# A new order of instructions for an adaptive-layer-norm block: the conditioning chain ahead of x1's statistics

## The chip, the cores and the metric

The kernel runs on one core of one Trainium2 chip. A core has five engines with a queue of instructions each: TensorE (PE in the profile; its weight loads are PEld), VectorE (DVE), ScalarE (ACT), GpSimd (POOL) and SyncE (SP), which here only issues DMA transfers. An engine works through its queue in order and waits at semaphores. The metric is the time of one execution on the device in microseconds (us).

## The reference

One transformer block with adaptive layer norm, on x of 2048 rows by 640, all in bf16:

```python
mod = (silu(c) @ w_mod).reshape(1, 6, 1, -1)          # c 1x640, w_mod 640x3840
sa, ca, ga, sb, cb, gb = (mod[:, i] for i in range(6))
h = layernorm(x) * (1 + ca) + sa
x = x + ga * attention(h)      # 32 heads of 20, causal, window 256, then @ wo
h = layernorm(x) * (1 + cb) + sb
x = x + gb * (sigmoid(h @ w_gate) * (h @ w_up)) @ w_down     # inner width 1536
```

Nothing of x can be modulated before c, the six products with w_mod and their way into per-partition or broadcast form are done: this is the conditioning chain.

## The kernel before, in words

x is worked on in eight chunks `a` of 256 rows, each of two blocks of 128 rows. For each chunk: load x; statistics and normalization (`ln_stats`, on VectorE, with the power on POOL; the normalization is L796); turning to hT, by TensorE for chunks 0 and 1 and by transposing DMAs (`transp_dma`, L803) afterwards; modulation of hT (`modulate`, L812, L813, L820, L821); projections to q, k and v (all plain matmuls are issued at L679, those with a tile position at L680); evacuation of q and k into a staging tile `stg` (four buffers; L895, L896) and transposing DMAs from there into QT and KT; scores, exp on ScalarE (L1016 for an edge set, L1042 for a main set), masks on POOL (L1051), the PV matmuls; normalization of the result through two stream transposes on VectorE (L1136, L1145), a trip through DRAM (`doc`) into oT; output projection, residual, second layer norm, transposing DMAs into h2T, its modulation, MLP and second residual. The gates ga and gb are multiplied into `wo` (L1316) and `wd`, the down weights (L1253, twelve slices, VectorE or POOL), once they have come back as a broadcast tile `gbc` through DRAM: gout writes the row, gin reads it back into all partitions. `gbc` holds first ga, then gb.

In the head, TensorE first runs warm-up matmuls on a zeroed tile (`warm`, L660). c arrives as a row, is turned by a matmul (ctr), halved (c_col, L646), put through tanh on ScalarE (cth, L647), becomes siluc on VectorE (L648) and silubc, repeated over columns (L651). `modA` then multiplies silubc with five slices of w_mod (wm0, held in the buffer of `wd`) in ten 64-column matmuls each; VectorE copies the result to mA (L759), and modulation of hT can begin. Between those products stand a few `fill` matmuls (L671).

**What sets the order.** Every operation is an `Op` with a list of allowed engines, a duration, dependences and, for a DMA, a size and a latency. The order is not computed at build time: the list `PLAN` holds one code for each operation, five times the operation's number plus the number of the engine (pe, act, dve, pool, sp). `schedule` walks it, puts each operation at the end of its engine's queue and keeps a model of time as it goes; the model decides which buffer of a pool a tile gets. `emit` then writes each engine's queue in that order, with a semaphore wait where a dependence crosses engines. So durations, latencies and the constants `DSAFE`, `MIXED` and `FETCH` reach the chip only through PLAN and through the choice of buffers. `DSAFE` is added, in the model, to the time from a DMA's landing to its use. A DMA on SP waits for its inputs at the head of SP's queue, and what stands behind it waits too.

Of the kernel before, what the change touches and what calls it, by code (L numbers as in the profile page):

```python
# [348 lines left out]
def c_pe(n):  # L349
# [4 lines left out]
    28, 222, 225, 81, 43, 33, 3, 258, 230, 8, 195, 13, 260, 89, 347, 352, 235, 240, 245, 250, 202, 357, 378, 91, 362,  # L354
    367, 372, 206, 212, 383, 388, 217, 397, 415, 104, 405, 411, 99, 109, 265, 114, 119, 275, 280, 129, 62, 393, 270,
    402, 430, 436, 68, 440, 447, 285, 426, 295, 305, 312, 461, 476, 452, 144, 124, 134, 149, 491, 290, 139, 457, 467,
    300, 420, 154, 472, 487, 482, 515, 23, 58, 520, 496, 615, 620, 526, 540, 546, 767, 600, 627, 500, 505, 511, 762,
    772, 777, 782, 787, 605, 611, 550, 555, 561, 530, 536, 73, 630, 637, 650, 565, 570, 576, 580, 655, 793, 798, 807,
    590, 802, 586, 640, 18, 1625, 850, 596, 662, 680, 665, 670, 1631, 1229, 174, 647, 159, 857, 840, 53, 687, 677,
    846, 700, 705, 712, 810, 48, 1640, 1646, 830, 1234, 179, 715, 730, 735, 78, 817, 837, 1242, 1237, 1257, 820, 1252,  # L360
    745, 826, 750, 756, 1247, 1638, 720, 1655, 1661, 169, 1262, 742, 727, 860, 865, 872, 925, 690, 696, 1653, 164,
    1120, 1529, 1268, 1534, 1273, 1287, 1537, 1725, 890, 1278, 1731, 930, 936, 1127, 1542, 1142, 875, 880, 897, 1552,
    1668, 910, 915, 887, 1557, 1740, 1746, 922, 1547, 1562, 1670, 1682, 1677, 960, 950, 965, 971, 957, 940, 1687,
    1755, 975, 1283, 946, 990, 1146, 1738, 997, 1568, 1010, 1015, 980, 1025, 319, 1761, 1060, 339, 1573, 1578, 1022,
    1040, 1753, 1046, 1587, 1134, 1154, 1299, 1692, 1030, 1036, 1294, 1322, 1065, 1071, 2805, 2811, 987, 1000, 1006,
    344, 194, 1105, 1110, 1583, 189, 1050, 1697, 1117, 1768, 1057, 1075, 1080, 2815, 1087, 1090, 2821, 900, 907, 1316,
    1311, 1308, 2838, 1303, 1770, 1782, 1777, 1139, 184, 1714, 1704, 1095, 2843, 1325, 1102, 1787, 2845, 2851, 1195,
    1202, 1217, 1395, 1400, 1340, 2833, 1406, 1345, 1719, 1709, 2709, 1351, 2868, 2873, 1172, 1495, 1792, 2875, 1375,
    1500, 1360, 2881, 1177, 1506, 1365, 1797, 1380, 1330, 2905, 2911, 1159, 1465, 1594, 1599, 2704, 1724, 1804, 1814,
    2903, 1387, 1337, 2732, 2727, 2898, 1470, 2863, 1510, 1430, 1435, 1515, 1522, 1476, 2888, 2933, 1441, 2928, 2935,  # L370
    1410, 1445, 1450, 1480, 2893, 2858, 2918, 2923, 2828, 2717, 1372, 1809, 1485, 2941, 1616, 1491, 1601, 2712, 1457,
    2722, 2737, 1415, 2945, 1182, 1187, 1192, 2743, 2748, 1819, 329, 1209, 1824, 1825, 1421, 1855, 2977, 1606, 1860,
    1867, 1621, 1830, 1837, 1974, 1359, 1870, 1875, 2951, 1840, 1845, 1611, 2982, 2987, 1464, 3025, 3031, 2500, 2505,
    1882, 1902, 1394, 2515, 2520, 2526, 2535, 1852, 2763, 2768, 38, 2753, 1429, 2779, 1989, 2550, 2540, 2758, 1221,
    3048, 2968, 1907, 1887, 2973, 1892, 1897, 2555, 2562, 1912, 2585, 2590, 2511, 3043, 2546, 2685, 2655, 2597, 2570,
    2958, 2690, 2696, 3055, 2963, 2575, 2992, 2582, 3078, 2620, 2625, 2632, 1918, 2774, 1923, 1927, 1932, 2605, 3061,
    2610, 2670, 2782, 2534, 2787, 2640, 2645, 3085, 3083, 3113, 2652, 2569, 2616, 2675, 2660, 2791, 2801, 3073, 3108,
    3220, 3053, 2796, 2682, 3235, 3225, 2604, 3091, 2639, 1214, 3038, 3103, 3098, 3068, 2667, 1944, 1939, 3240, 324,
    3246, 3231, 3130, 3135, 2997, 3009, 3115, 3120, 3127, 3420, 3150, 3165, 3155, 3162, 2037, 1992, 3141, 3426, 3170,
    3176, 3200, 3205, 1997, 1947, 3430, 3211, 3467, 1951, 1961, 1958, 1967, 3185, 3285, 3290, 2042, 3297, 3458, 3453,  # L380
    3462, 2047, 2002, 2075, 2080, 2085, 2090, 2095, 2050, 2055, 2060, 2065, 2070, 3436, 3448, 2110, 2115, 2120, 3472,
    3477, 1979, 2007, 2125, 2101, 2130, 4105, 4133, 3004, 4128, 2161, 2135, 2140, 2145, 3014, 1164, 1169, 3019, 2150,
    4111, 3255, 2155, 3319, 334, 3324, 1984, 4584, 3190, 3260, 3266, 2107, 2167, 2012, 4135, 4158, 4141, 3482, 3494,
    4163, 4579, 2170, 2195, 2175, 2200, 2205, 3504, 2210, 2180, 4123, 2185, 2190, 2215, 3489, 2221, 3197, 4165, 3327,
    2227, 3347, 3342, 3352, 3332, 3337, 2255, 2260, 3300, 2265, 4607, 4171, 4602, 3270, 3275, 3281, 4153, 4188, 4193,
    4148, 3443, 3305, 3311, 4178, 3499, 3358, 4183, 4118, 3363, 3368, 4195, 2230, 2235, 2240, 2270, 2245, 3378, 2275,
    2250, 2290, 4201, 2281, 2295, 2300, 2305, 2310, 2341, 4205, 4211, 4592, 2315, 2320, 2287, 3373, 2325, 3383, 2330,
# [983 lines left out]
```

## Time and profile before

| | us |
|---|---|
| three timed runs | 326.62, 326.90, 328.47 |
| median | 326.9 |
| profiled execution | 330.35 |
| its span, first to last instruction | 328.6 |
| PE / DVE / ACT / POOL busy in it | 320.4 / 204.5 / 212.8 / 187.6 |
| mean granted TensorE clock | 0.995 |

Where the profile is a page of sums, a row of a group gives line, engine, operation, destination and sources, count, busy time, mean duration and the idle time ahead of it with what ended it. A row of the timeline gives the start from the beginning of the span, the length, and the same names; in brackets stand the idle time before it and who ended that. SPq and ACTq are DMA issues. A busy TensorE is not TensorE at its peak: ends of matmuls are modelled, and warm-up and fill matmuls count as busy.

### The profile page before, as it was taken

The numbers are of one execution on the slowest core, as the hardware profiler recorded it, in microseconds if no ns is written. First come the engines' busy times: TensorE is split into PE (matmuls) and PEld (weight loads), VectorE is DVE, ScalarE is ACT, GpSimd is POOL, SyncE is SP. The second block draws the span as 40 slices with busy tenths as digits, with TensorE's granted clock in tenths as the row PEclk, the third lists the DMA queues.
The fourth block names the chain that finished last, engine by engine and source line by source line (L and its number), as shares of the span: only waits on it lengthen the run. The fifth ranks groups of instructions, "written<-read, shape, count | busy, mean of one in ns | idle before, by whom it ended". The sixth has DMA issues, their size and how long they took to land.

```text
span 328.6 us, 11961 instructions
## 1 busy us (share of the span) xinstructions
PE 320.4 (97%) x5045; PEld 239.7 (73%) x5045; DVE 204.5 (62%) x421; ACT 212.8 (65%) x229; POOL 187.6 (57%) x325
## 2 busy tenths in 40 slices
PE   5999999989999999999999999999999999999996
PEld 2666766666777777776777778777888777887885
DVE  4589878549776666874476637463846366745422
ACT  1589999586977667877586767585686667220220
POOL 3148777564967767867675665748572859201000
PEclk9899999999999999999999999999999999999999
DMA  7996989999763562424553211374030213122201
GB/s 246 372 323 167 308 167 218 161 150 349 207 92 70 115 142 67 94 63 108 128 77 60 56 25 28 61 119 119 16 90 19 65 42 77 28 60 41 82 0 42
DMA packets 73007, 38.20 MB, mean 116 GB/s; under 512 B 46586, under 2 KB 71674, under 8 KB 72954
## 3 DMA queue, kind: packets, MB, share of 16 engines
q1 hardware_dynamic: 71936, 36.29, 46.7%
q10 hardware_dynamic: 1018, 1.15, 1.1%
q8 instruction: 40, 0.66, 0.8%
q14 instruction: 13, 0.11, 0.1%
HBM read 21.30 MB, written 5.25 MB: 81 GB/s over the span
## 4 chain that ended last, share of the span: by engine, by line
PE 89%; DMA 7%; DVE 2%; issue 1%; ACT 1%; SPq 0%; ACTq 0%; DVEq 0%
PE M L679 73%; PE S L680 8%; PE M L680 6%; DMA QT<-stg 2%; DMA hT<-x 2%; DMA gbc<-gate 2%; DMA x<-in_A_x_dram 1%; PE S L679 1%; ACT E L1016 1%; PE S L671 1%; SPq L803 0%; DVE V L896 0%; DVE wd L1253 0%; DVE st L774 0%; DVE T L1136 0%
## 5 line engine op out<-in xcount | busy, mean ns | idle before, releaser
L1051 POOL TENSOR_SCALAR_AFFINE_SELECT E<-E 128x512 bf16<-128x512 bf16 x224 | 141.8, 664 | 63.7 <-PE S L680 23.5
L1042 ACT ACTIVATE E<-S 128x2048 bf16<-128x2048 f32 x56 | 105.0, 1875 | 35.4 <-PE S L680 34.2
L679 PE MATMUL M<-h2T,wu 128*128 128x256 bf16 x480 | 70.5, 273 | 0.5 <-DVE T L1136 0.5
L679 PE MATMUL M<-h2T,wg 128*128 128x256 bf16 x480 | 65.6, 273 | 0.0
L679 PE MATMUL M<-wd,hh 128*128 128x320 bf16 (+2 forms) x396 | 56.9, 295 | 0.0
L679 PEld LDWEIGHTS M<-h2T,wu 128*128 128x128 bf16 x480 | 44.8, 98 | 9.1 <-DVE T L1136 0.8
L679 PEld LDWEIGHTS M<-h2T,wg 128*128 128x128 bf16 x480 | 46.0, 98 | 6.7
L1270 ACT ACTIVATE sig<-M 128x512 f32<-128x512 f32 x48 | 28.2, 596 | 32.1 <-PE M L679 31.0
L1272 DVE SCALAR_TENSOR_TENSOR hh<-sig,M 128x512 bf16<-128x512 f32 x48 | 32.2, 678 | 26.6 <-ACT sig L1270 17.4
L679 PEld LDWEIGHTS M<-wd,hh 128*128 128x128 bf16 x396 | 37.3, 98 | 14.0
L1291 DVE TENSOR_TENSOR x<-M,x 128x320 bf16<-128x320 f32 (+2 forms) x33 | 15.5, 480 | 35.4 <-PE M L679 35.1
L680 PE MATMUL S<-QT,KT 20*64 20x64 bf16 (+4 forms) x1856 | 34.9, 211 | 0.1
L680 PEld LDWEIGHTS S<-QT,KT 20*128 20x128 bf16 (+1 forms) x1856 | 22.1, 98 | 17.6 <-issue 9.2
L1016 ACT ACTIVATE E<-S 128x2048 bf16<-128x2048 f32 x14 | 26.3, 1877 | 10.2 <-PE S L680 10.2
L774 DVE BATCH_NORM_STATS2 st<-x 128x6 f32<-128x320 bf16 x64 | 28.6, 478 | 3.5 <-DMA x<-in_A_x_dram 3.2
L1136 DVE STREAM_TRANSPOSE T<-M 128x512 f32<-128x512 f32 x32 | 21.6, 700 | 14.5 <-PE S L680 13.5
L679 PE MATMUL M<-wk,hT 128*128 128x320 bf16 x160 | 26.6, 299 | 1.1 <-DVE V L896 1.1
L679 PE MATMUL M<-wq,hT 128*128 128x320 bf16 x160 | 26.9, 299 | 0.6 <-DMA QT<-stg 0.5
L679 PE MATMUL M<-wv,hT 128*128 128x320 bf16 x160 | 27.2, 300 | 0.0
L679 PE MATMUL M<-wo,oT 128*128 128x320 bf16 x160 | 25.4, 299 | 0.0
L680 PE MATMUL M<-E,V 128*32 128x256 bf16 (+1 forms) x960 | 23.0, 246 | 0.1
L680 PEld LDWEIGHTS M<-E,V 128*32 128x32 bf16 x960 | 19.1, 97 | 4.3 <-issue 2.7
(82 smaller groups left out, 321.5 us busy)
## 6 DMA issues: line engine op xcount, KB each, us to landing
x<-in_A_x_dram SPq DMA_DIRECT2D x23, 160.0 KB, 3.7
doc<-On SPq DMA_DIRECT2D x64, 40.0 KB
wd<-in_w_mod_dram SPq DMA_DIRECT2D x6, 320.0 KB
wd<-in_B_w_down_dram SPq DMA_DIRECT2D x4, 480.0 KB
out_dram<-x SPq DMA_DIRECT2D x11, 160.0 KB, 2.1
wu<-in_w_mod_dram SPq DMA_DIRECT2D x5, 320.0 KB, 6.7
oT<-doc SPq DMA_DIRECT2D x8, 192.0 KB, 2.7
wg<-in_B_w_gate_dram SPq DMA_DIRECT2D x2, 576.0 KB
```

Source lines behind the costliest of these rows:

```text
L671: ins = e.matmul(p_S.aps[0][:, 3, :], Eall[:, 0:128], Eall[:, 128:640], start=True, stop=True)
L679: return e.matmul(o, l, r, start=st, stop=sp, skip_group_check=True)
L680: return e.matmul(o, l, r, start=st, stop=sp, tile_position=tp, skip_group_check=True)
L774: A("dve", lambda e, g, bi=bi, j=j: e.bn_stats(v(bi * 12 + j * 6, 6), src[bi].ap[:, j * 320:(j + 1) * 320]), 0.48, reads=[src[bi].r()], wr ...
L1016: A("act", lambda e, eng: e.activation(G.ap[:], Sp.ap[:], ACT.Exp, scale=SM_SCALE), 1.876, reads=[Sp.r()], writes=[G.r()], prio=3, tag=f"e ...
L1042: A("act", lambda e, eng: e.activation(wide()[:, :, 64:320], Sp.ap[:].rearrange("p j (t c) -> p (j t) c", c=256), ACT.Exp, scale=SM_SCALE) ...
L1051: A("pool", lambda e, eng, ap=ap, inp=inp, pat=pat, base=base, cm=cm: e.affine_select(ap(), inp(), pattern=pat, compare_op=ALU.is_ge, fill ...
L1136: A("dve", lambda e, g, h=h: e.transpose(T1.ap[:, 512 * h:512 * h + 512], X[h].ap), 0.694, reads=[X[h].r()], writes=[T1.r(h)], prio=3.5, t ...
L1270: A("act", lambda e, g, pg=pg, sg=sg: e.activation(sg.ap[:], pg.ap[:], ACT.Tanh, scale=0.5), c_act(512), reads=[pg.r()], writes=[sg.r()], ...
L1272: A("dve", lambda e, g, pu=pu, sg=sg, f0=f0: e.scalar_tensor_tensor(out=hh.ap[:, f0:f0 + 2, :], in0=sg.ap[:].rearrange("p (a b) -> p a b", ...
L1291: A("dve", lambda e, g, ps=ps, bi=bi, c0=c0, n=n: e.tensor_tensor(x1[bi].ap[:, c0:c0 + n], ps.ap[:, 0:n], x1[bi].ap[:, c0:c0 + n], op=ALU. ...
```

## The change

All 2134 operations stay as they are; three warm-up operations are added (nine instead of six, seventeen matmuls of 512 columns instead of eleven), so the numbers of later operations move by three. The model's figures are altered, and PLAN is replaced by another list for them:

```diff
 PLAN = [
-    28, 222, 225, 81, 43, 33, 3, 258, 230, 8, 195, 13, 260, 89, 347, 352, 235, ...
+    13, 222, 225, 81, 3, 8, 273, 275, 89, 362, 104, 195, 367, 202, 372, 393, ...
...
-DSAFE = 0.2
+DSAFE = 1.0
...
 FETCH = [
-    4.30, 15.19, 23.69, 31.86, ...
+    -5, 15.19, 23.69, 31.86, ...
...
-            dlat=2.95 if pool is p_x1 and b < 4 else 2.24)
+            dlat=(2.95, 4.6, 2.95, 2.95)[b] if pool is p_x1 and b < 4 else 2.24)
...
-                    (2.2 if hi - lo == 640 else 1.12), writes=..., prio=prio, tag=k)
+                    (2.2 if hi - lo == 640 else 1.12), writes=..., prio=prio, tag=k,
+                tmin=2.4)
...
-    load_bulk(wm_ap[0], wm_src[:, :, 0:1280], Rm[0], 0.88, 0.2, "wm0", dlat=2.89)
+    load_bulk(wm_ap[0], wm_src[:, :, 0:1280], Rm[0], 0.88, 0.2, "wm0", dlat=4.0)
...
-    for i in range(6):
-        o = A("pe", warm if i < 5 else lambda e, g: warm(e, g, 1), 1.03 if i < 5 else 0.52, ...)
+    for i in range(9):
+        o = A("pe", warm if i < 8 else lambda e, g: warm(e, g, 1), 1.03 if i < 3 else 0.6 if i < 8 else 0.3, ...)
...
-        last["s"] = [with_pv(f"edge{a}", sc, 0.36, rd, [G, Sp], before, 3)]
+        last["s"] = [with_pv(f"edge{a}", sc, 0.54, rd, [G, Sp], before, 3)]
```

The codes of PLAN, turned back into names, give the queues. Those that the text below speaks of (number behind a name: chunk; x0, x1: blocks of chunk 0; qkt: a transpose from stg into QT or KT; atr, btr: transposes into hT and h2T; amodu, bmodu: their modulations; wds: one scaling of wd):

```
VectorE, head
  before: stats x0, c_col, aggr x0, stats x1, aggr x1, siluc, silubc, norm x0, memset, norm x1, hT evac, mA, modulations
  after:  stats x0, c_col, aggr x0, memset, siluc, silubc, norm x0, stats x1, aggr x1, memset, hT evac, norm x1, mA, modulations
TensorE, head
  before: warm x2, ctr, ident product, warm x4, turn x0, modA 0 1, fills, turn x1, modA 2 3 4, fills, projections
  after:  warm, ident product, ctr, warm x5, turn x0, warm, modA 0 1, warm x2, modA 2, fill, turn x1 (part), fill, modA 3 4, fill, turn x1 (rest), fills, projections
POOL, modulations of chunk 0:  before none;  after two of the ten
SP, ahead of the first gate row
  before: x6, x7, wg0 first part, wm3 first part, gout 0, wu0 first part, atr2, atr2, wm3 second part, wm2, wm2, gin 0
  after:  x6, x7, wm3, wm3, wg1 first part, gout 0, wu0 first part, atr2, atr2, wm2, wm2, gin 0
SP, from oT of chunk 0 on
  before: oT0, wd0, qkt2 x4, atr4, wd3, atr4, qkt3 x4, gin 1, btr0, btr0, wg0 rest
  after:  oT0, qkt2 x2, wd0, qkt2 x2, atr4, atr4, gin 1, qkt3, wd3, qkt3 x3, btr0, btr0, wg0 rest
ACT, modulations of chunk 4:  before three of five (DVE two);  after all five
x10, x11, x13 loads:  before issued by SP;  after by ACT
wds:  before all twelve on DVE;  after nine on DVE, three on POOL (2 and 3 among chunk 2's first masks, 7 later)
```

Instructions listed for ScalarE go from 236 to 230, for VectorE from 421 to 429, for POOL from 313 to 310, for SP from 205 to 206.

More of the change, by code (lines that the diff above doesn't have):

```diff
@@ L628, in load_w3 @@
             dma(lambda lo=lo, hi=hi: W3[k][:, :, lo:hi], lambda lo=lo, hi=hi: wqkv_src[:, :, i * D + lo:i * D + hi],
-                    (2.2 if hi - lo == 640 else 1.12), writes=[R_w3[k][lo // 320]] if halves else R_w3[k], prio=prio, tag=k)
+                    (2.2 if hi - lo == 640 else 1.12), writes=[R_w3[k][lo // 320]] if halves else R_w3[k], prio=prio, tag=k,
+                tmin=2.4)
     x0 = {}
@@ L662, in build @@
     wprev = []
-    for i in range(6):
-        o = A("pe", warm if i < 5 else lambda e, g: warm(e, g, 1), 1.03 if i < 5 else 0.52, prio=90, reads=[R_z], extra=wprev, tag="warm", writes=[R("w")])
+    for i in range(9):
+        o = A("pe", warm if i < 8 else lambda e, g: warm(e, g, 1), 1.03 if i < 3 else 0.6 if i < 8 else 0.3, prio=90, reads=[R_z], extra=wprev, tag="warm", writes=[R("w")])
         wprev = [o]
```

227 rows, old and new, of tables (FETCH, PLAN) are left out of this document.

## The prediction

> **What bounds the kernel now.** I read the page first, then the list of waits by engine, then sums over stretches, then the chain of waits and the timeline where those pointed.
>
> ```profile
> span 328.6 us, 11961 instructions
> ...
> PE 320.4 (97%) x5045; PEld 239.7 (73%) x5045; DVE 204.5 (62%) x421; ACT 212.8 (65%) x229; POOL 187.6 (57%) x325
> ...
> PEclk9899999999999999999999999999999999999999
> DMA  7996989999763562424553211374030213122201
> ```
>
> TensorE carries the time: 320.4 of 328.6 us, and the only digit of its clock row below 9 is the second, 8.2 to 16.4 us. DMA is busy at 0.6 to 0.9 for the first ten slices (82 us) and slack afterwards. Where TensorE is idle at all, the sums over stretches tell (stretch, its length, busy time of PE, PEld, DVE, ACT, POOL with counts, granted clock, DMA share, GB/s), and the waits name who ended it:
>
> ```profile
> 4.30:5.50 1.20, 1.20 (x6) 0.39 (x4) 0.04 (x1) 0.11 (x1) 0.82 (x2) 1.00 0.94 361
> 5.50:7.70 2.20, 0.09 (x2) 0.04 (x2) 2.06 (x7) 0.00 (x0) 0.23 (x1) 1.00 1.01 361
> 7.70:11.00 3.30, 3.30 (x39) 2.75 (x40) 0.69 (x3) 0.84 (x2) 1.00 (x2) 0.50 1.09 355
> 49.00:77.00 28.00, 25.80 (x427) 17.44 (x415) 19.03 (x45) 21.02 (x30) 16.98 (x31) 1.00 1.06 192
> 77.00:326.00 249.00, 249.00 (x3916) 192.18 (x3914) 148.18 (x287) 155.35 (x152) 142.44 (x234) 1.00 0.35 79
> ```
> ```profile
> PE M L679 <- DVE x L796: 2.1, 1, 2.1
> PE S L660 <- DVE E L655: 1.3, 1, 1.3
> PE M L679 <- DVE V L896: 1.1, 1, 1.1
> PE M L679 <- DMA QT<-stg: 0.5, 1, 0.5
> PE M L679 <- DVE T L1136: 0.5, 1, 0.5
> ```
>
> So there are two places to win. In the head TensorE idles 2.1 us for the normalized x0, and then runs 3.30 us at half clock. Between 49 and 77 us it idles 2.2 us in three waits. After 77 us it is busy in 249.00 of 249.00 us: there only the amount of matmul work counts, and a new plan can only lose.
>
> **The change part by part.** The constants (margin after a landing, edge cost, landing times, prefetch table) act only through the order of instructions that PLAN lists; the sole new instructions are six 512-column warm-up matmuls. Every cost is a matter of order.
>
> *Head.* The rows of before:
>
> ```profile
> 1.24 2.31 SPq L574 DMA_DIRECT2D wd<-in_w_mod_dram  x5
> ...
> 1.38 0.37 ACTq L574 DMA_DIRECT2D x<-in_A_x_dram  x1
> ...
> 3.21 0.89 DVE L774 BATCH_NORM_STATS2 st<-x 128x6 f32<-128x320 bf16 x2 [1.97 <-DMA x<-in_A_x_dram]
> ...
> 4.20 0.21 ACT L647 ACTIVATE cth<-c_col 128x5 f32<-128x5 bf16 x1 [1.14 <-DVE c_col L646]
> ...
> 4.75 0.58 POOL L783 TENSOR_TENSOR st<-st,mhalf 128x1 f32<-128x1 f32 x1
> ...
> 5.57 0.89 DVE L774 BATCH_NORM_STATS2 st<-x 128x6 f32<-128x320 bf16 x2 [1.22 <-DMA x<-in_A_x_dram]
> ...
> 6.62 0.11 DVE L648 SCALAR_TENSOR_TENSOR siluc<-cth,c_col 128x5 bf16<-128x5 f32 x1
> 6.76 0.49 DVE L651 COPY silubc<-siluc 128x320 bf16<-128x320 bf16 x1
> ...
> 7.17 0.44 DVE L796 TENSOR_SCALAR x<-x,st 128x640 bf16<-128x640 bf16 x1
> ...
> 7.66 0.71 PE L679 MATMUL M<-ident,x 128*128 128x128 bf16 x5 [2.11 <-DVE x L796]
> ...
> 8.17 1.27 PE L679 MATMUL S<-silubc,wd 128*128 128x64 bf16 x20
> ...
> 11.92 0.17 DVE L759 COPY mA<-S 128x10 f32<-128x10 f32 x1 [0.63 <-PE S L679]
> ...
> 12.76 1.47 PE L679 MATMUL M<-wq,hT 128*128 128x320 bf16 x8
> ```
>
> VectorE waits until 5.57 for x1, with siluc, silubc and the normalization of x0 queued behind x1's statistics, though their inputs (cth at 4.41, x0's power at 5.33) are there. In the new order they come first: siluc 4.5, silubc done 5.1, x0 5.4 to 5.85, and x0's transposes at 5.9 instead of 7.66. The six added warm-up matmuls (1.2 us, as the six of the row 4.30:5.50) stand behind x0's transposes and the first two slices of the modulation product, where TensorE would wait for x1 anyway. x1's statistics slip from 5.57 to 5.85 and end at 7.0; two small steps on POOL and its normalization follow by 8.5, ahead of the last slices: no loss.
>
> What ends last then is w_mod's fifth slice. x0, x1 and five slices are 1.97 MB; at the 361 GB/s of these rows, with the first bytes about 2.3 us in, they have moved at 7.8, and a landing is seen some 1.5 us later (estimate 9.4, from x0: 160 KB issued at 0.79, seen at 3.21). The last two slices' twenty matmuls take half of that 1.27 at full clock, so mA is copied near 10.2, and by the 0.84 us from mA to the first projection, that one comes at 11.2 (range 11.0 to 11.6, as one modulation moves to POOL behind another): 1.5 us earlier than 12.76.
>
> But that price holds for an execution that lost its clock. A before without the half-clock stretch finds the same last slice and gains about 0.1. The three times, 326.62, 326.90 and 328.47, lie 1.6 to 1.8 us apart, about half of the 3.30 us; I therefore take the median run as one that mostly kept its clock. Ends 0.1 and 1.5; I take **-0.4**, nearer the low end by two times of three.
>
> The rule beside this row: the Trainium skill, "TensorE: Matmul & The Clock Gate", section "What's actually happening", drops the clock after at least one idle window of about 3.4 us. The trace disagrees: here 2.2 us with 0.09 busy, after 1.20 fully busy, were enough. By the rule the clock would not have dropped, the head would gain 0.1, and the sum would be 324.8.
>
> *Middle, 49 to 77 us.* The chain of waits (start, length, what), and the timeline of SP, VectorE, ScalarE and TensorE there:
>
> ```profile
> 49.33 7.33 DMA QT<-stg
> ...
> 59.64 6.33 DMA hT<-x
> ...
> 69.10 5.02 DMA gbc<-gate
> ```
> ```profile
> 59.01 0.59 SPq L574 DMA_DIRECT2D wd<-in_B_w_down_dram  x1
> 59.64 3.41 SPq L803 DMA_TRANSPOSE hT<-x  x1
> 63.59 1.24 SPq L803 DMA_TRANSPOSE QT<-stg  x1
> ```
> ```profile
> 65.99 1.58 ACT L820 ACTIVATE hT<-hT,mA 128x256 bf16<-128x256 bf16 x3 [1.74 <-DMA hT<-x]
> ...
> 67.09 1.52 PE L679 MATMUL M<-wk,hT 128*128 128x320 bf16 x10 [1.11 <-DVE V L896]
> ...
> 74.21 1.42 DVE L1253 TENSOR_TENSOR wd<-wd,gbc 128x640 bf16<-128x640 bf16 x3 [1.96 <-DMA gbc<-gate]
> ```
>
> First wait (0.5, at 56.79): chunk 3's projection wants a staging buffer back from chunk 2's transpose, which was issued behind a 480 KB slice of w_down and took 7.33 us. The new order issues two of the four transposes ahead of that slice. Second (1.1, at 67.09): hT of chunk 4 has one transpose ahead of the next w_down slice and one behind; the latter takes 6.33 us and ends just before the modulation at 65.99. The new order has both ahead. Third (0.5, at 76.57): VectorE stands for gbc with the scaling of w_down at the head of its queue, h2T's modulation behind. The new order issues that gate row before chunk 3's transposes, some 6 us earlier against TensorE's work, so the stand disappears. All three gone: **-2.2**, by the stretch row.
>
> *What comes back.* (a) The w_down slice now lies between the first and second transposes of chunk 3, so chunk 4's second projection wants a buffer that lands behind it. Issue to landing behind such a slice is 6 to 7 us in the rows above; with the slice issued near 57 the buffer comes at 64.5 to 65.2, and TensorE asks at 65.0 in the same frame: 0 to 1.0. (b) All five modulations of chunk 4 are now on ScalarE (three, in 1.58, before), 2.6 us in series. Counting the matmuls that stand ahead of it in the new order, TensorE comes to chunk 4's first projection near 63.2 in this execution's frame (67.09 less 1.5 of the head, less the waits before it, and some matmuls now behind it); the modulations are covered while hT lands by 60.5, and with both transposes ahead of the slice I expect 58 to 59. (c) Three of the twelve scalings of w_down go to POOL, two of them among the masks of chunk 2. No row has that form there:
>
> ```profile
> L1253 DVE TENSOR_TENSOR wd<-wd,gbc x12: 426/485/934, 74.2 to 96.5; 128x640 bf16<-128x640 bf16 x12
> ```
> ```profile
> L793 POOL TENSOR_SCALAR x<-x,st 128x640 bf16<-128x640 bf16 x6 | 5.2, 873 | 2.2 <-PE M L679 1.9 <-POOL st L788 0.3
> ```
>
> At least 0.87, at most about four of VectorE's 0.485; I take 1.4, nearer the low row as both read bf16. With it two scalings, 2.8 us, fit among the masks with about 0.7 to spare before chunk 2's first PV matmuls: 0 to 0.8 lost. The Trainium skill ("GPSIMD Engine Reference", section "4.1 Engine selection") puts an elementwise operation of two inputs at about twice VectorE's time: 1.0 here as an estimate, nothing of (c) comes back then, and the sum would be 324.3; no row shows it. Of (a) to (c), 0 to 3, I take **+0.2**.
>
> Three DMA issues for later x blocks move from SP to ScalarE near 60 to 66 us, at the 0.37 of x1's issue each; ScalarE waits 1.74 for hT there, which covers them, else 1.2 is lost. SP's gate row near 25 us gets one more transfer ahead of it: its wait there is for a VectorE result, DMA drains less meanwhile, and no wait of TensorE in the list hangs on the transposes of chunk 2 behind it: 0. Everything after 77 us shifts as a whole: 0, with a loss of up to 0.3 where the last chunk's way from output projection to MLP has about 0.9 us less of TensorE's work in between.
>
> **Sum.** The profiled execution took 330.35, 1.75 outside its span and 3.45 above the median of the runs; the same differences are set against the median: 326.9 - 0.4 - 2.2 + 0.2 = **324.5**.
>
> **The rivals.** *The waits move, they do not go.* The queue of transfers, at share 1.06 from 49 to 77 us, sets these landings, not the order; TensorE then waits its 2.2 elsewhere: 326.5. For it: the share. Against: each wait hangs on one transfer behind one slice. *Slower, by (b).* If hT of chunk 4 lands later than 60.5 in the new run, each us is a us of TensorE, since five modulations in series follow; from a landing at 62.9 the whole gain of 2.4 is spent, and at 65.7, about where it lands now, the time is 324.5 + 5.2 = 329.7. For it: 6.33 us for that one transpose. Against: both are now ahead of the slice. *The head pays in full.* If the median run did lose its clock: 326.9 - 1.5 - 2.2 + 0.2 = 323.4.
>
> **How the numbers follow.** Forecast 0.53, head in full 0.15, waits move 0.20, slower 0.12. A measurement here tells 0.5% (1.6 us) from no change. Faster by more (under 325.3): 0.53 and 0.15, 0.68. Within: 0.20. Slower (over 328.5): 0.12. The range of 8 in 10 runs from 322.4 (head in full, nothing comes back, the last slice 0.8 sooner than estimated) to 327.0 (waits moved, with 0.5 for (c)). The forecast's own range is 323.2 to 325.3.
>
> **What would show it.** Right: siluc before x1's statistics, x0's transposes near 5.9, no half clock from 7.7 to 11, first projection near 11.2; between 49 and 72 us TensorE idle under 1 us, no stand for gbc, first matmul of chunk 0's MLP 3 to 4.5 us earlier than 76.57. Wrong: half clock again in the head (a stretch too idle), a new wait on QT, KT or hT transposes between 60 and 70, PV waiting on masks near 87, or any wait after 77.

## The result, and the profile after

The changed kernel takes 331.8 us (median of four executions, 331.54 to 333.49) where the kernel before takes 327.0 on the same chip: a ratio of 1.0122, interval 1.0072 to 1.0171. A later set of seven gave 1.0097 (1.0062 to 1.0132). It is slower by 1.0 to 1.2%, 3 to 5 us; forecast were 2.4 us the other way. Executions of both kernels scatter over several us (the kernel before from 325.65 to 331.3 over all sets), so what follows goes by the ratios on record with their intervals, and by single profiles for where the time lies. These ratios are not plain quotients of two medians, which here would be 1.015 and elsewhere differ by up to 0.2%.

The page of the changed kernel, its sums over stretches (length, busy time of PE, PEld, DVE, ACT, POOL with counts, granted clock, DMA share, GB/s), and its list of waits:

```profile
span 330.2 us, 11979 instructions
...
PE 321.5 (97%) x5051; PEld 238.9 (72%) x5051; DVE 208.0 (63%) x429; ACT 211.8 (64%) x224; POOL 189.2 (57%) x322
...
PEclk9999999999999999999999999999999999999999
```
```profile
49.00:77.00 28.00, 23.90 (x402) 16.02 (x401) 19.17 (x42) 18.39 (x24) 16.92 (x31) 1.00 1.06 199
77.00:150.00 73.00, 72.92 (x1248) 54.52 (x1247) 50.41 (x105) 56.64 (x60) 56.26 (x89) 1.00 0.58 121
150.00:326.00 176.00, 175.90 (x2663) 136.74 (x2661) 97.53 (x184) 99.55 (x93) 86.49 (x141) 1.00 0.26 59
```
```profile
PE M L681 <- DMA KT<-stg: 1.8, 2, 1.4
PE M L681 <- ACT E L1018: 1.6, 1, 1.6
PE S L662 <- DVE E L657: 1.3, 1, 1.3
PE M L681 <- DMA oT<-doc: 0.6, 1, 0.6
```

The half clock of the head is gone from this execution: the clock row is 9 throughout. After 77 us TensorE is idle for 0.18 us in 249. Between 49 and 77 us it is idle for 4.1 us, where the profile of before had 2.2. Where, its timeline says, and the timeline of SP what it waited for:

```profile
52.88 1.79 PE L681 MATMUL M<-wo,oT 128*128 128x320 bf16 x12 [0.63 <-DMA oT<-doc]
60.64 0.43 PE L681 MATMUL M<-wk,hT 128*128 128x320 bf16 x2 [0.34 <-DMA KT<-stg]
68.82 1.52 PE L681 MATMUL M<-wq,hT 128*128 128x320 bf16 x10 [1.44 <-DMA KT<-stg]
72.92 0.43 PE L681 MATMUL M<-wk,hT 128*128 128x320 bf16 x2 [1.56 <-ACT E L1018]
```
```profile
56.47 4.07 SPq L805 DMA_TRANSPOSE hT<-x  x2
60.65 0.52 SPq L575 DMA_DIRECT2D gbc<-gate  x1
61.28 1.23 SPq L805 DMA_TRANSPOSE QT<-stg  x1
62.56 0.62 SPq L575 DMA_DIRECT2D wd<-in_B_w_down_dram  x1
63.28 1.28 SPq L805 DMA_TRANSPOSE KT<-stg  x1
64.66 2.83 SPq L805 DMA_TRANSPOSE QT<-stg  x1
67.67 1.23 SPq L805 DMA_TRANSPOSE KT<-stg  x1
```

The two long waits are for staging buffers of chunk 3: projection q of chunk 4 at 68.82 for the one that the transpose issued at 63.28 empties (landed from 68.56, behind wd3, which landed from 67.56), projection k at 72.92 for the one of 67.67. Of that transfer's sixteen parts one landed at 71.36, just as TensorE asked, and the other fifteen from 72.66 to 72.78: most of the 1.56 is this pause of 1.3 within one transfer, for which no cause was found. That the list names ScalarE there is the end of an exp at the same moment; the semaphore is that of the transpose.

Set against a second profile of before, one at full clock (the first run below), the loss can be laid out by stage. For each kind of TensorE operation I took the usual time from its start to the next start (median over both traces), summed it over all useful operations begun so far (no warm-up, no fills) and took that from the clock time: by how much TensorE then stands behind an unbroken run.

```
us behind, at            14     49     62     80     end
before, repeat          8.08   3.81   3.40   3.65   1.11
changed                 8.98   5.16   5.09   7.65   5.77
difference              0.90   1.35   1.69   4.00   4.66
```

So, in these two profiles, 0.9 is lost in the head, 0.8 from there to 62 us, 2.3 between 62 and 80 us, and 0.7 afterwards.

### The profile page after: what moved, and what is told of

It reads as the page before. It is cut to its first block, busy times and chain, and to the rows that moved or that the text cites. A ratio compares the mean times of both kernels' runs of the same rounds, so it can differ in the third digit from the quotient of the medians.

```text
span 330.2 us, 11979 instructions
## 1 busy us (share of the span) xinstructions
PE 321.5 (97%) x5051; PEld 238.9 (72%) x5051; DVE 208.0 (63%) x429; ACT 211.8 (64%) x224; POOL 189.2 (57%) x322
## 4 chain that ended last, share of the span: by engine, by line
PE 88%; DMA 7%; DVE 2%; ACT 1%; issue 1%; SPq 0%; POOL 0%; DVEq 0%
PE M L681 71%; PE S L682 8%; PE M L682 7%; DMA KT<-stg 3%; PE S L662 2%; DMA hT<-x 1%; DMA oT<-doc 1%; DMA doc<-On 1%; DVE On L1147 1%; ACT E L1018 1%; PE S L681 1%; DVE Tn L1145 0%; SPq L575 0%; DVE stg L898 0%; ACT hT L814 0%
## 5 line engine op out<-in xcount | busy, mean ns | idle before, releaser
L681 PE MATMUL M<-h2T,wu 128*128 128x256 bf16 x480 | 69.1, 273 | 0.1
L681 PE MATMUL M<-h2T,wg 128*128 128x256 bf16 x480 | 68.6, 273 | 0.0
L681 PE MATMUL M<-wd,hh 128*128 128x320 bf16 (+2 forms) x396 | 57.4, 295 | 0.0
L681 PEld LDWEIGHTS M<-h2T,wg 128*128 128x128 bf16 x480 | 45.4, 98 | 7.5 <-DVE x L1293 0.2
L681 PEld LDWEIGHTS M<-h2T,wu 128*128 128x128 bf16 x480 | 45.2, 98 | 7.7 <-issue 0.3
L681 PEld LDWEIGHTS M<-wd,hh 128*128 128x128 bf16 x396 | 37.3, 98 | 14.1 <-DVE stg L898 0.2
L681 PE MATMUL M<-wk,hT 128*128 128x320 bf16 x160 | 28.1, 299 | 2.0 <-ACT E L1018 1.6
L681 PE MATMUL M<-wq,hT 128*128 128x320 bf16 x160 | 27.2, 299 | 1.8 <-DMA KT<-stg 1.4
L681 PE MATMUL M<-wv,hT 128*128 128x320 bf16 x160 | 27.2, 299 | 0.0
L681 PE MATMUL M<-wo,oT 128*128 128x320 bf16 x160 | 26.2, 299 | 0.6 <-DMA oT<-doc 0.6
L898 DVE CAST stg<-M 128x320 bf16<-128x320 f32 x35 | 16.6, 481 | 11.3 <-PE M L681 11.2
```

The lines of the kernel that those rows point to most:

```text
L681: return e.matmul(o, l, r, start=st, stop=sp, skip_group_check=True)
L898: return e.tensor_copy(dst(), src())
```

## The experiments

Each kernel is one of the two with codes moved in PLAN; the diffs give the queues in names. But for the unchanged repeats, a table holds every buffer number at that of its base, so that only the named order differs; the table moves line numbers (L681 becomes L719, L679 becomes L718). Ratios are to the kernel before on the same chip; the number in front of them is a median in us.

**What a typical execution of before is.** Unchanged, ten executions:

> The kernel before, unchanged, once more. Its profiled execution took 330.35, its median is 326.9: 3.4 us that the profile of before has and the median has not. Theory A: the profiled execution had lost its clock in the head (1.5) and had most of the three waits between 49 and 77 us (2.2) as an accident; a typical execution has granted clock 1.000, first projection near 11.3 us, and idle time between 49 and 77 us under 1 us. Then the prediction's 2.2 was never there to gain. Theory B: the waits are in every execution (idle 2.2 there again), and the difference lies elsewhere.

Median 328.1, ratio 1.0006 (0.9969 to 1.0044). The profiled execution took 327.3, at clock 1.000, with the first projection at 10.74. Its stretch from 49 to 77 us, and the longer of the two long waits there:

```profile
49.00:77.00 28.00, 26.53 (x442) 18.77 (x440) 20.26 (x44) 20.88 (x32) 16.95 (x31) 1.00 1.04 206
```
```profile
64.86 1.38 PE L679 MATMUL M<-wk,hT 128*128 128x320 bf16 x9 [0.73 <-DVE V L896]
```

The other is 0.71 at 51.77 for oT. So neither theory as it stands. The stretch is idle for 1.47, not under 1 (theory A) and not 2.2 (theory B); of the three waits on which the prediction set 2.2, only one is there, hT of chunk 4, with 0.73. This is one profile. In other kernels below that are as before up to that point, the first of the three waits, that for a staging buffer near 55 us, is back with 0.5 to 0.7 (0.48 in b_wd3, 0.52 in b_gin, 0.68 in b_sp, 0.50 in b_best2) and absent in two (b_best, b_head2). So some 0.7 was there to be gained in these executions, not 2.2. And the head of before, with its clock, is at its first projection at 10.7, earlier than the 11.3 of theory A and than the 11.2 forecast for the new head.

**The head alone.** A first attempt kept POOL waiting on VectorE: the schedule of this kernel makes some POOL operations wait for the VectorE operation ahead of them in PLAN, and the list put together from two orders had such waits on later work. It took 336.9, ratio 1.0263, and so does not tell what the head is worth.

> Only the head of the change: all instructions that the changed kernel starts before 11.7 us, in its order and on its engines (nine warm-up operations, siluc ahead of x1's statistics, two modulations on POOL), and from the first projection on the order and buffers of before. If the head is harmless or better: 326.5 to 327.0, clock 1.000. If the head loses 0.5 (first projection 11.76 in the changed kernel against some 11.3 for a before at full clock): 327.3 to 327.6. If all of the 4.8 came from the head: 331.

```profile
PE M L719 <- POOL h2T L861: 4.6, 3, 2.5
```

The second attempt puts the changed kernel's queues up to 11.7 us in front of those of before, with the order of before between VectorE and POOL from there on:

```diff
 all engines, up to 11.7 us
-  order and engines of before
+  order and engines of the changed kernel (nine warm-up operations, two modulations on POOL)
```

> The head of the change alone again, this time with the locks between VectorE and POOL in the order of before from the first projection on (in the first attempt POOL waited there for later VectorE work, which is what cost it 9 us). TensorE's useful work by 14 us stood 0.9 us further back in the changed kernel than in the repeat of before (warm-up work at half clock until 6.9, w_mod's fifth slice). Theory (the new head is worth nothing on average: its first projection came between 10.7 and 11.8 us, by when the clock was granted and the slice landed, before's between 10.7 and 10.9): 0.2 to 0.8 slower than before, 0.1 to 0.25%. Rival (the prediction's: x0 earlier, 0.1 to 0.4 faster, and no execution with a lost clock): 0.03 to 0.12% faster, the slow tail of before (330 and more, clock 0.995) gone.

327.8 against 327.9: ratio 1.0000 (0.9977 to 1.0022). This shows no gain and no loss, but an interval of 0.7 us to either side does not rule out the forecast 0.4. The profile says more: its first projection was at 11.69, 0.95 later than in the repeat of before, and the only wait left between 49 and 77 us was 0.76 for oT: that for hT of chunk 4 was gone, so part of what the head lost came back where TensorE had waited anyway (behind by 0.73 more at 14 us, by 0.52 at 80).

Why it is no earlier, the changed kernel's TensorE shows in part:

```profile
2.69 4.38 PE L662 MATMUL S<-E 128*128 128x512 bf16 x10
6.91 0.44 PE L681 MATMUL M<-ident,x 128*128 128x128 bf16 x5
...
9.68 0.75 PE L681 MATMUL S<-silubc,wd 128*128 128x64 bf16 x20
...
11.76 0.97 PE L681 MATMUL M<-wq,hT 128*128 128x320 bf16 x6 [0.30 <-POOL hT L815]
```

Ten warm-up matmuls take 4.38 us, 0.43 each, at half clock, which was first granted in full at 6.87; x0 had been normalized by 5.7, but its transposes stand behind them. Over the profiles of both heads the first grant came between 4.3 and 7.5 us. In the new head TensorE's own chain runs without a break from there to mA when the grant is late. But over the thirteen profiles with the new head x0's transposes start from 5.8 to 6.9, and even where they come at 5.8 (b_head and a_wd3s) the first projection comes at 10.7 to 10.8, level with before. There the way from mA to the first projection takes 1.29 to 1.30, where before needs 0.84: two modulations in series on POOL use up what mA had won. The Trainium skill ("TensorE: Matmul & The Clock Gate", section "What's actually happening") calls the window over which the clock is decided free-running, and variable from run to run; that the moment of the grant differs between executions, these traces show.

Two edits tried to win the head back:

```diff
 a_nopool, modulations 0 and 9 of chunk 0
-  POOL: 9, 0
+  VectorE: 0 first after mA; ScalarE: 9 last
```

> The changed kernel with the two modulations of chunk 0 that POOL has (0 and 9) back on VectorE (first after mA) and ScalarE (last), as before had them. In the changed kernel the first projection comes 1.29 us after mA (10.47 to 11.76), in before 0.84 (9.90 to 10.74). Theory (two modulations in series on POOL put it off): 0.8 to 0.9 again, time 331.4. Rival (the late point is mA itself, set by w_mod's slices and x1's last transposes in TensorE's queue): from mA on 1.2 to 1.3 again, 331.8.

332.5, ratio 1.014 (1.0109 to 1.017). From mA to the first projection it took 0.85, as the theory said (1.29 before), but the next ones waited for it: the sixth operation after it came 3.28 after mA, in the changed kernel 3.14. No gain.

```diff
 a_tiny (with wd3 late, as in a_wd3s below), warm-up
-  nine operations, seventeen matmuls of 512 columns
+  nine operations, eleven matmuls of 512 columns and three of 64
```

> The changed kernel with wd3 and its scalings late (the run that gave 329.43), and with its warm-up work cut to that of before: eleven matmuls of 512 columns, and the last three of the nine operations one matmul of 64 columns each. Theory (TensorE's first full clock came between 4.3 and 7.5 us in the runs so far, and the first projection of the changed head followed it, 10.74 to 11.76, since TensorE's own chain of warm-up matmuls is the last to end there; before has 10.74 and 10.92 whenever): first projection 10.5 to 11.0, and the time 0.4 to 0.7 under the 329.43: 328.7 to 329.0. Rival (the head's last event is the landing of w_mod's fifth slice): no change, 329.4; or, with less warm-up, the half clock comes back in some executions and the median rises over 329.5.

328.8, ratio 1.0024 (0.9996 to 1.0052), where the run without this edit had 1.0069 (1.0044 to 1.0094) on another chip. The time came out as expected, its reason did not: in this profile the first projection was at 11.77, with TensorE waiting for the fifth slice:

```profile
9.69 0.76 PE L719 MATMUL S<-silubc,wd 128*128 128x64 bf16 x20 [0.57 <-DMA wd<-in_w_mod_dram]
```

So the slice (landed 9.64 here, 8.24 in the changed kernel) and the grant can each bound the new head, and which of them ends last changes from run to run. What the shorter warm-up is worth is not settled by one profile.

**wd3 in the changed kernel.** First the slice alone, behind both h2T transposes:

```diff
 SP
-  gin 1, qkt3 0, wd3, qkt3 1, qkt3 2, qkt3 3, btr0, btr0
+  gin 1, qkt3 0, qkt3 1, qkt3 2, qkt3 3, btr0, btr0, wd3
```

> The changed kernel with slice wd3 of w_down (480 KB) issued behind both h2T transposes of chunk 0 (btr0) instead of between chunk 3's first and second transposes; every buffer as in the changed kernel. Theory late staging: the transposes behind it land 2 to 4 us earlier, both waits at 68.8 and 72.9 go (3.0): 328.8 to 330. Rival, order: no change, 331.8. Should the scaling of wd3 now make VectorE or POOL stand, 331 to 333.

332.5, ratio 1.0142 (1.0089 to 1.0195; two of its four executions had a granted clock below 1, 0.990 and 0.995): no gain in time, yet both waits for staging buffers were gone. Chunk 3's last three transposes landed from 65.1, 66.4 and 67.7 (68.6, 70.1 and 72.7 in the changed kernel). In their place VectorE stood for wd3 with an evacuation behind, and TensorE for that:

```profile
73.14 1.02 DVE L1293 TENSOR_TENSOR wd<-wd,gbc 128x640 bf16<-128x640 bf16 x2 [3.03 <-DMA wd<-in_B_w_down_dram]
```
```profile
75.28 0.85 PE L719 MATMUL M<-wv,hT 128*128 128x320 bf16 x5 [1.66 <-DVE stg L936]
```

Then with that stand taken away:

```diff
 VectorE (with wd3 as above)
-  wds 0, ..., wds 9, wds 10, bmodu0 4, wds 1, ..., wds 11
+  wds 0, ..., bmodu0 4, wds 1, ..., wds 9, wds 10, wds 11
```

> The changed kernel with wd3 behind btr0, as in the run before, and with the two scalings of it that VectorE did first (wds 9 and 10) just ahead of the third (wds 11), so that VectorE does not stand for it. Theory (wd3 between the transposes makes the staging buffers late): with no stand left, the 1.44 and 1.56 at 68.8 and 72.9 are gone and nothing takes their place: 328.5 to 329.5, idle of TensorE between 49 and 77 us about 1 to 1.5. Rival (the middle is limited by the issue of transposes on SP and by the other moved transfers, wd3 only shows where): a wait of 1.5 or more appears somewhere else before 80 us, 331 to 332.5.

329.4, ratio 1.0069 (1.0044 to 1.0094): some of the loss is gone, up to half of it; this interval still overlaps that of the changed kernel's repeat, on another chip. A wait of 0.83 is left, and ScalarE's timeline says why: it stood for chunk 0's h2T with an evacuation of chunk 4 behind, whose PSUM buffer TensorE wanted.

```profile
72.71 0.45 PE L719 MATMUL M<-wq,hT 128*128 128x320 bf16 x2 [0.83 <-ACT stg L935]
```
```profile
71.24 1.09 ACT L860 ACTIVATE h2T<-h2T,shB,scB 128x256 bf16<-128x256 bf16 x2 [1.30 <-DMA h2T<-x]
```

With the two modulations off POOL besides, no better:

> Both edits together: wd3 behind the transposes with its scalings late, and no modulation of chunk 0 on POOL. If the loss of 3.8 is head (0.5 to 0.9) and staging (3.0), this stands level with before: 328.0 to 328.8. Rival: 331 or more, if the loss comes from the rest of the order.

330.6, ratio 1.0083 (1.0057 to 1.0109). This run and a_nopool differ in wd3 and its scalings alone, and ran on one chip: 330.6 against 332.5, intervals that just touch (1.0057 to 1.0109 and 1.0109 to 1.0170). That 1.9 us is the plainest measure of what wd3 among the transposes costs in this order.

**The transfers on the kernel before.** Now the other way round, one part of the change at a time. All four base on before's `atr4, wd3, atr4, qkt3 0, qkt3 1, qkt3 2, qkt3 3, gin 1, btr0, btr0`:

```diff
 SP
 b_wd3
+  atr4, atr4, qkt3 0, wd3, qkt3 1, qkt3 2, qkt3 3, gin 1, btr0, btr0
 b_gin
+  atr4, atr4, gin 1, qkt3 0, wd3, qkt3 1, qkt3 2, qkt3 3, btr0, btr0
 b_sp: as b_gin, and on ScalarE x11 behind evv3, x13 and x10 behind evqk4 (SP had them near 77 us)
 b_best
+  atr4, atr4, qkt3 0, qkt3 1, qkt3 2, qkt3 3, gin 1, btr0, btr0, wd3   (wds 9 to 11 fourth to sixth)
```

> The kernel before with one thing of the change alone: wd3 issued between chunk 3's first and second transposes instead of between chunk 4's two hT transposes. Theory: the second to fourth staging buffers come 3 us later, TensorE waits for them between 66 and 73 us, while the wait for hT of chunk 4 (0.7 in the repeat of before) goes: 1 to 3 us slower, 329 to 331. Rival (only together with the moved loads of x10, x11, x13 and the gate row): 327.3 to 328.3, the wait for hT gone and none in its place.

> The kernel before with the transfers of the change and nothing else: gate row (gin 1) ahead of chunk 3's transposes, wd3 between the first and the second of them, x11, x13 and x10 issued by ScalarE at the change's places (behind evv3 and behind evqk4). The run with wd3 alone cost nothing. Theory (it is the sum of what was put ahead of the last three transposes that makes them late): staging buffers 1.5 to 3 us later than in the repeat of before (65.4, 66.5, 67.9), TensorE waits 1.5 to 3 between 64 and 72 us, 329 to 330.5. Rival (the transfers alone do no harm; TensorE's own new order of chunks 3 and 4, or the later qkt2, is needed for it): 327.3 to 328.2.

> The kernel before with wd3 between chunk 3's first and second transposes and the gate row ahead of them, the loads of x10, x11 and x13 left where before has them. wd3 alone cost nothing (staging waits 1.0 in its profile), wd3, gate row and the three loads together 0.38%. If the early loads are the part that tips it (x11 160 KB issued just ahead of the first transpose, x13 and x10 behind the third): 327.5 to 328.3, level with before, waits for staging buffers between 64 and 73 us under 1. If the gate row is: 329 to 329.6.

```
                          ratio to before            chunk 3's 2nd transpose, TensorE asks, waits
wd3 alone                 0.9996 (0.9966 to 1.0026)      66.31      66.46    0.18
wd3 and gate row          1.0041 (1.0016 to 1.0067)      67.87      66.50    1.69
the same and three loads  1.0038 (1.0010 to 1.0066)      67.76      66.53    1.54
```

(First landing of its sixteen parts, by the semaphore events.) The gate row tips it, by the profiles more than by the ratios, whose intervals overlap and which come from different chips (the wait goes from 0.18 to 1.69 and 1.54; four of b_gin's twelve executions had a granted clock of 0.995, but none of b_sp's); the loads of x10, x11 and x13 cost nothing that can be measured. SP's timeline of b_wd3, of b_gin, and TensorE's row of the latter:

```profile
59.75 1.31 SPq L842 DMA_TRANSPOSE QT<-stg  x1
61.12 0.58 SPq L613 DMA_DIRECT2D wd<-in_B_w_down_dram  x1
61.83 1.25 SPq L842 DMA_TRANSPOSE KT<-stg  x1
63.18 2.11 SPq L842 DMA_TRANSPOSE QT<-stg  x1
65.47 1.23 SPq L842 DMA_TRANSPOSE KT<-stg  x1
```
```profile
59.73 1.03 SPq L613 DMA_DIRECT2D gbc<-gate  x1
60.88 1.26 SPq L842 DMA_TRANSPOSE QT<-stg  x1
62.19 0.56 SPq L613 DMA_DIRECT2D wd<-in_B_w_down_dram  x1
62.85 1.24 SPq L842 DMA_TRANSPOSE KT<-stg  x1
64.20 2.59 SPq L842 DMA_TRANSPOSE QT<-stg  x1
66.97 1.23 SPq L842 DMA_TRANSPOSE KT<-stg  x1
```
```profile
68.18 1.52 PE L718 MATMUL M<-wq,hT 128*128 128x320 bf16 x10 [1.69 <-DMA KT<-stg]
```

With wd3 alone the second buffer comes back as TensorE asks: its parts land from 66.31 to 66.51, TensorE asks at 66.46 and waits 0.18. The slice had used up the slack to the last, and cost nothing in time (its profile has a wait of 0.85 at 58.62 for a buffer of chunk 2 besides). The gate row then puts the first transpose off by 1.1 in issue and 1.9 in landing (62.74 to 64.64), the second by 1.6, and the wait grows by 1.5.

The same for the best of it, without any slice or gate row among the transposes, in two sets of twelve:

> The kernel before with what the runs showed to be of use: wd3 behind both h2T transposes of chunk 0, so that both hT transposes of chunk 4 and all four of chunk 3 have no 480 KB slice ahead of them, and its three scalings fourth to sixth among the twelve, not first. In the repeat of before TensorE waits 0.73 at 64.86 for hT of chunk 4. Theory: that wait goes and nothing comes in its place: 0.5 to 0.8 faster than before, 0.15 to 0.25%. Rival: VectorE or POOL stand for the scalings, and the same 0.7 is lost at chunk 0's MLP or at chunk 2's masks: no difference.

> The kernel before with wd3 behind btr0 and its scalings fourth to sixth, once more: the first time gave 0.9983 (0.996 to 1.0006), a profile without the wait for hT of chunk 4. Gain real: 0.997 to 0.999, interval below 1. Not real: 1.000 or more.

0.9983 (0.996 to 1.0006) and 0.9992 (0.9966 to 1.0018). The wait for hT of chunk 4 is gone in both profiles, and one of 0.48 and 1.11 at chunk 0's MLP has come, near 75 us. Level with before; nothing that beats it was found.

**The gate row in the changed kernel, and both.**

> The changed kernel, unchanged, on the chip of the next run and with more executions: 331.2 to 332 beside a before of 327.5 to 328, ratio 1.011 to 1.013, if nothing depends on the chip; the first four executions gave 1.0122.

```diff
 a_gin, SP
-  gin 1, qkt3 0, wd3, qkt3 1, qkt3 2, qkt3 3, btr0, btr0
+  qkt3 0, wd3, qkt3 1, qkt3 2, qkt3 3, gin 1, btr0, btr0      (VectorE: wds 0 one place later)
 a_late, SP
+  qkt3 0, qkt3 1, qkt3 2, qkt3 3, gin 1, btr0, btr0, wd3      (wds 9 and 10 late as well)
```

> The changed kernel with the gate row (gin 1) behind chunk 3's transposes, where before has it, and the first scaling that needs it one place later on VectorE; wd3 stays between the transposes, x11 is still issued by ScalarE near 60 us. In the runs so far a transpose behind a plain copy landed 0.9 to 1.05 us after that copy, whatever its size. Theory (any copy ahead does it): x11 takes the gate row's part, qkt3 0 lands 1.0 after x11 and the later ones as before; at most 0.8 gained: 331.0 to 331.8. Rival (the gate row itself is what is slow, a broadcast read of one row): the transposes land 1 to 1.5 sooner, TensorE's waits of 1.44 and 1.56 shrink by as much each: 329.3 to 330.3.

> The changed kernel with both transfers back behind chunk 3's transposes: gate row (gin 1) behind the fourth, wd3 behind btr0, and the scalings that wait for them correspondingly late. wd3 alone took 0.53% of the ratio away, the gate row alone 0.45% (of 1.0097 to 1.0122). If the two add up (each copy in between costs its own landing): 1.000 to 1.003. If they are two ways to the same 2 us (either alone is enough to keep the waits away): 1.005 to 1.007, and what is left over before lies in the rest of the order, which stood 0.5 to 0.9 us further back from 80 us to the end in every profile of this order.

The unchanged repeat gave 1.0097. With the gate row late: 1.0052 (1.0022 to 1.0081), 2 us less, waits for staging buffers 0.21 and 0.60 instead of 0.90 and 2.00. The time is of the rival's size, though the two intervals overlap and the executions at full clock alone lie 1.3 us apart (329.7 and 331.0). The landings are the theory's: x11 landed at 62.0 and the first transpose 0.9 behind it, at 62.91, and the first three came 0.6 to 0.8 sooner than in the repeat of the changed kernel (62.91, 66.17 and 67.05 against 63.75, 66.75 and 67.61). The fourth came 2.0 sooner (69.28 against 71.28), of which 1.35 is a pause within that transfer that the repeat had (parts from 69.93, the rest at 71.28) and this profile had not. With both late: 1.0096 (1.0064 to 1.0128), although no wait for a staging buffer is left. Seven of its twelve executions had a granted clock of 0.995, and the profile shows where (same columns as above, and TensorE's rows):

```profile
71.01:74.42 3.41, 1.71 (x70) 1.16 (x59) 1.61 (x4) 1.61 (x4) 0.67 (x2) 1.00 0.80 250
74.42:77.84 3.42, 3.42 (x16) 2.17 (x15) 3.32 (x7) 2.37 (x3) 1.87 (x2) 0.50 1.08 373
```
```profile
72.58 0.34 PE L720 MATMUL M<-E,V 128*32 128x128 bf16 x6 [0.69 <-issue]
...
74.27 0.60 PE L719 MATMUL M<-wq,hT 128*128 128x320 bf16 x2 [1.01 <-ACT stg L935]
```

After two idle stretches of 0.69 and 1.01 within 2.4 us, the second ending at 74.27, the clock fell to half for one window of 3.4 us. The five executions with the full clock have a median of 329.64, 1.006 of the kernel before: together the two edits show no more than either alone.

**What is left over.**

```diff
 a_evk (a_tiny besides), ScalarE
-  exp2 0, bmodu0 3, bmodu0 0, evqk4 3
+  exp2 0, evqk4 3, bmodu0 3, bmodu0 0
```

> The changed kernel with wd3 and its scalings late and the warm-up work of before (the run that gave 1.0024), and with one evacuation of chunk 4 (evqk4 3) on ScalarE ahead of chunk 0's two modulations of h2T (bmodu0 3 and 0) instead of behind them. In every profile with the staging wait gone ScalarE stood for h2T's landing at 71.2 to 72.8 with that evacuation behind, and TensorE waited 0.83 to 1.22 for its PSUM buffer. Theory: that wait goes, 0.8 to 1.2 faster than the run with 1.0024: 0.998 to 1.001. Rival: the wait moves on to the h2T modulations and chunk 0's MLP: 1.002 to 1.003.

1.0025 (0.9996 to 1.0054), no change: the wait moved to the next projection, 1.09, since VectorE stands for the same h2T with another evacuation behind.

```profile
73.57 0.85 PE L719 MATMUL M<-wv,hT 128*128 128x320 bf16 x5 [1.09 <-DVE stg L936]
```

A last run: the three x loads back on SP near 77 us.

> The changed kernel with the loads of x10, x11 and x13 back on SP, behind its last bulk load near 77 us, as before had them; every buffer as in the changed kernel. Theory late staging: these 480 KB are transferred among chunk 3's transposes and put off the last of them (landing 72.8, before 71.1); without them TensorE's wait at 72.9 (1.56) goes and the one at 68.8 (1.44) shrinks: 329.5 to 330.5. Rival, order: TensorE merely asks earlier than the transposes can be issued on SP (1.2 to 2.8 each): no change, 331.8.

345.3, ratio 1.0526 (1.0476 to 1.0575), since the new order of VectorE has chunk 5's statistics ahead of work that TensorE needs, and stood for x10 (15.8 us). As a time it says nothing of the loads. Its profile does: without them the waits for chunk 3's staging buffers are still there, with 1.17 and 0.98, so the loads are not their cause, as b_sp says too.

```profile
PE M L720 <- DVE stg L936: 12.7, 1, 12.7
```

## Why the prediction was wrong

*Head, -0.4 with ends 0.1 and 1.5.* Measured: no change (1.0000, to within 0.7 us, which does not exclude 0.4). Two to one between 0.1 and 1.5 makes 0.57, not 0.4. That the median of before mostly kept its clock was right. The failing step is the lower end: "a before without the half-clock stretch finds the same last slice and gains about 0.1". Such a before has its first projection at 10.7 to 10.9 (six profiles), the new head at 10.7 to 11.8. What was mis-sized is before's own point: 11.2 was about right for the new head, but before at full clock was already at 10.7. Siluc and x0's normalization did come as forecast (4.35 and 5.24); x0's transposes came not at 5.9 but, in this profile, at 6.91 behind warm-up matmuls at half clock, which were counted as free. The sum of 324.8 that went with the Trainium skill's rule is nearer to the result than 324.5, but by luck: the profile of before did lose its clock after a window of 3.4 us in which TensorE was busy for 1.3 (4.26 to 7.68).

*Middle, -2.2.* The three waits of the first profile went as told, or nearly: TensorE took chunk 3's first q without a wait at 56.99 (0.34 for its fourth buffer, at 60.64), waited 0.14 for chunk 4's hT, and not at all for the stand for gbc. But the base was one execution at the slow end of the scatter: the repeat's profile had 0.73 of them, other kernels as before up to there 0.5 to 0.7, of the first wait. Profiled time 3.45 above the median was noted and put aside in "the same differences are set against the median"; a saving of waits can't be larger than what the median execution waits. That one term put some 1.5 us too much into the gain.

*Coming back, (a).* This is the step that failed first of all. "With the slice issued near 57 the buffer comes at 64.5 to 65.2, and TensorE asks at 65.0": the slice was issued at 62.56, since SP came to it only behind the second half of chunk 2's transposes, both of chunk 4's and the gate row; its transpose took 5.3 from issue to landing, the buffer came at 68.6, TensorE asked at 67.4. So the time behind the slice was near what was taken (6 to 7); the moment of the slice's issue was wrong by 5.6 us. The fourth buffer (1.56, of which 1.3 is the pause between the parts of its transfer) was not looked at. Forecast 0 to 1.0; measured 3.0 in the profile. The prediction had named this sign of being wrong, a new wait on such a transpose between 60 and 70, and it came. And the gate row ahead of the transposes was booked as a gain only, the end of the stand for gbc; put on the kernel before together with wd3 it costs 0.4% (1.0041 and 1.0038, both intervals above 1), where wd3 alone costs nothing (0.9996).

*(b)* hT of chunk 4 landed at 62.8, not 58 to 59, but TensorE, late by then, waited 0.14 for it; in the profile of a_nopool 1.79. *(c)* The scalings on POOL:

```profile
L1255 DVE TENSOR_TENSOR wd<-wd,gbc x9: 481/484/911, 70.1 to 99.5; 128x640 bf16<-128x640 bf16 x9
L1255 POOL TENSOR_TENSOR wd<-wd,gbc x3: 1394/1396/1398, 76.6 to 96.0; 128x640 bf16<-128x640 bf16 x3
```

1.40 as taken, 2.9 times VectorE's; the Trainium skill's factor ("GPSIMD Engine Reference", section "4.1 Engine selection") of about two is too low for this form. No PV waited for masks. The three loads by ScalarE cost nothing, as said.

*After 77 us, 0 with up to 0.3.* From 80 us to the end TensorE lost 0.7 more than in the repeat of before, against the 0.3 allowed. Only 0.18 of it shows as idle time; where the rest lies was not found, and that it is the named chain of the last chunk is not shown.

*The rivals.* "Waits move, they do not go" was right that waits would come up at other transposes. Its cause, that the load of the queue and not the order sets the landings, does not stand: from b_wd3 to b_gin one move in the order put the landings off by 1.6 to 1.9 us. And its 326.5 moved 2.2, not what the new order adds. "Slower, by (b)" had the sign and the wrong transfer. By the ratios, the transfers around chunk 3 account for about half of the loss (1.0097 to 1.0122 down to 1.0052 and 1.0069 when either is put back; 1.9 us by the pair on one chip). The other half stays open: the shorter warm-up came with 0.45% (of two chips), the stand for h2T only moved, and some 0.7 us lies behind 80 us. Part of the loss may be clock: of the changed kernel's eleven executions four had a granted clock of 0.995, of the kernel before's some 140 only twelve. The four of the repeat's set with the full clock have a median of 330.97 beside 328.59 for before, 1.007 where all seven give 1.010. In which stretch the clock is lost there, no profile shows.

## What to carry to other kernels

A wait in one profile is worth only what the median execution waits there: profile the kernel more than once before a saving is summed, above all where the profiled time lies off the median. When an order moves copies in among transposing DMAs that return buffers, follow every buffer to its landing and set it beside the moment TensorE asks, all four and not the first; and ask when the queue will come to that copy, not only how long it takes. A move that costs nothing may have used the last of the slack, and the next one pays in full. Behind a wait that was taken away there stood, here, the next engine that waits at the head of its queue for a late transfer.

## What the runs showed of the hardware

In these runs a transposing DMA never overtook the copy ahead of it. In the twenty profiles there are 32 transposes issued on SP directly behind a slice of w_down. Each landed after the slice, first part behind the slice's last by 0.8 to 2.4 us; from last part to last part it was 0.9 to 1.2 in 24 of them, 1.35 and 1.6 in two, and 2.4 to 2.6 in six. With no copy between, chunk 3's transposes landed 2.9 to 3.6 us after their issue (a_late); behind wd3 the second one took 5.3 (the changed kernel, 63.28 to 68.56). The "0.9 to 1.05" of one expectation above came from fewer pairs. The Trainium skill ("DMA: Bandwidth & Descriptors", section "Two DMAs through the same engine are not ordered") grants no such order; the landings here had it.

Nor did all parts of a transfer land together: of the transpose at 67.67 one part landed at 71.36 and the others from 72.66, with the DMA engines at a share of 0.07 from 71.4 to 72.6. Such a pause hit the same transpose in a_again (69.93, the rest at 71.28), b_gin (70.00, 72.09), b_sp (70.58, 72.08) and a_xlate (69.12, 70.57), and other transfers in b_wd3 (the gate row, 69.06, 70.97), b_again (h2T, 70.24, 71.38) and a_wd3 (a load of x, 69.67, 70.98); in a_gin there was none. It comes near 70 us in both orders, and what causes it was not found.

The clock fell here without a whole idle window. The stretches of 3.4 us before a window at half clock had TensorE busy for 1.3 us (before, 4.26 to 7.68), 1.42 (b_head, 250.36 to 253.78) and 1.71 (a_late, 71.01 to 74.42); a stretch busy for 1.93 of 3.40 kept the clock (a_xlate, 70.70 to 74.10).
